# Splitting the first keys two and five, and moving the first FFN chunks behind the fourth slot's value product

## The chip, the cores and the metric

The kernel runs on one core of one Trainium2 chip. TensorE (PE) multiplies matrices and transposes, VectorE (DVE) and ScalarE (ACT) move and transform what it leaves in PSUM, GpSimd (POOL) and SyncE (SP) mostly issue DMAs. The metric is device time of one execution, in microseconds (us), as the median of several runs.

## The reference

```python
q, k, v: (8, 12, 448, 64)          # batch, heads, tokens, head size
scores = q @ k.transpose(0, 1, 3, 2) / sqrt(64) - log(448)
attn   = sigmoid(scores)
x      = (attn @ v).transpose(0, 2, 1, 3).reshape(8 * 448, 768)
out    = (relu(x @ w_gate) * (x @ w_val)) @ w_out      # 768 -> 1536 -> 768
```

Attention has a sigmoid in the place of a softmax, so no row needs a sum before its values are multiplied. The FFN that follows is gated: a gate product, a value product, their elementwise product, and a product down.

## The kernel before, in words

Everything is computed in fp16 with sums in fp32. The order of each engine's instructions is the order of the program text: no scheduler moves anything, and semaphores between the engines follow from the tiles. TensorE's queue therefore runs strictly in the order in which the Python code issues.

A batch has 12 heads, taken in 3 groups of 4. Tokens of a head are cut into 7 chunks of 64. Two heads lie beside each other on the 128 rows, and the transposed queries and keys of a group are held in one tile (`qkT`: 7 chunks of keys, then 7 of queries). Scores are products of 64 x 64 tiles (L238); ScalarE turns them into probabilities `PT` (L186); the value product `pv` (L256) sums over the 7 key chunks, and DVE copies it to `xT` (L183), the FFN's input. Transposes are TensorE matmuls with an identity (L203) into a PSUM bank and a DVE copy to `qkT` (L210).

Batch 0 is treated apart, since nothing else can run beside it at first. Its queries are cut in two halves, of chunks 0 to 3 (256 columns for a head) and 4 to 6 (192). That gives six *slots*, half by group: slots 0 to 2 are groups 0 to 2 with the first half of the queries, slots 3 to 5 the same groups with the second. A slot has four *units* `(i, u)`: units 0 to 2 are two key chunks each, unit 3 is the last one. A unit is scores into one of two score buffers (`pairp`, two PSUM banks each) and one sigmoid over both heads. A buffer must be read by ScalarE before the next but one unit may be written. Four other PSUM banks (`bank`) go round for everything else: transposes, value products, FFN chunks, filler.

What TensorE does between the units is written by hand in the dictionary `after`: what is issued behind unit `(i, u)`. Such work is transposes for later groups, filler matmuls on zeros (`keep_warm(count, columns)`), value products of earlier slots, and FFN chunks. An FFN chunk of the first query half (`gv`, 256 columns) is six matmuls for the gate and six for the value of one of 12 column blocks of 128; DVE takes the maximum with 0 and multiplies. `ffn_mix(1)` issues the next entry of `gv_queue`; the queue's entries for the first half are chunk 0, chunk 1, and one entry of chunks 2 and 3 together (`gv_two`: both gates, then both values).

The first loads are plain fp32 transfers into `ysb` buffers, cast on the chip: keys 0 to 3 of group 0 by SP, queries 0 to 3 and then keys 4 to 6 by ScalarE's queue. All else is loaded and cast by POOL's DMAs in a fixed order: keys and queries of groups 1 and 2, the rest of the queries, the values, then weights (`load_gv`) for chunks 0 and 1, for 2 and 3, batch 1's first group, and so on.

After slot 5 comes batch 1, with scores of all 448 queries at once (the 64x448 matmuls of L238), mixed with the remaining FFN chunks; from there on both versions of the program issue the same.

Of the kernel before, what the change touches and what calls it, by code (L numbers as in the profile page):

```python
# [17 lines left out]
def kernel(  # L18
# [10 lines left out]
    nc = tc.nc  # L29

    B, H, S, D = q.shape
# [3 lines left out]
    P = 128  # L35
    NCH = S // 64
    NDC = DM // P
# [3 lines left out]
    HALVES = ((0, QCUT), (QCUT, NCH))  # L41
# [34 lines left out]
    def bank(name, shape=(P, 512), dtype=FP32):  # L76
        pool, tag = free[0]
        free.rotate(-1)
        return pool.tile(list(shape), dtype, tag=tag, name=name)

    def bank16(name):
        return bank(name, (P, 1024), FP16)
# [35 lines left out]
            )  # L118


    KCUT = 4
    first32 = []
    for src, c0, c1, eng in ((k, 0, KCUT, nc.sync), (q, 0, QCUT, nc.scalar), (k, KCUT, NCH, nc.scalar)):
        ysb = ysbp.tile([P, DM], FP32, tag="ysb", name="ysb")
# [15 lines left out]
    wg = wpool.tile([P, NDC, DF], FP16, name="wg")  # L140
    wv = wpool.tile([P, NDC, DF], FP16, name="wv")
# [26 lines left out]
    xT_tiles = {}  # L168
    hT_tiles = {}

    def keep_warm(count, n=S):
        ps = bank("warm_ps")
        for _ in range(count):
            nc.tensor.matmul(ps[:, 0:n], zeros[:, 0:P], zeros[:, 0:n], start=True, stop=True)
# [14 lines left out]
    def qkT_of(b, g):  # L189
        if (b, g) not in qkT_tiles:  # L190
            qkT_tiles[(b, g)] = qkTp.tile([P, TW, P], FP16, tag="qkT", name="qkT")
        return qkT_tiles[(b, g)]

    def pe_transposes(b, g, ti, c0=0, c1=NCH):
        transposed(b, g, ti, c0, c1)()

    def transposed(b, g, ti, c0, c1):
        t16 = in_tiles[b][ti]
        qkT = qkT_of(b, g)
        trt = bank16("trt")  # L200
        for c in range(c0, c1):
            for h in range(2):
                nc.tensor.transpose(  # L203
                    trt[64 * h : 64 * h + 64, c * P : (c + 1) * P],
                    t16[:, 2 * g + h, c * D : (c + 1) * D],
                    ident[:],
                )

        def copy(a0=c0, a1=c1):
            nc.vector.tensor_copy(  # L210
                qkT[:, ti * NCH + a0 : ti * NCH + a1, :].rearrange("p c x -> p (c x)"),
                trt[:, a0 * P : a1 * P],
            )

        return copy
# [92 lines left out]


    def gv(b, q0, qn, f, act_relu):  # L310
        gv_out(b, q0, qn, f, act_relu, [gv_product(b, q0, qn, f, i) for i in range(2)])

    def gv_two(b, q0, qn, f):
        ps = [[gv_product(b, q0, qn, f + u, i) for u in range(2)] for i in range(2)]
        for u in range(2):
            gv_out(b, q0, qn, f + u, False, (ps[0][u], ps[1][u]))

    def gv_product(b, q0, qn, f, i):
        ps = bank(("g_ps", "v_ps")[i])
        for dc in range(NDC):  # L320
            nc.tensor.matmul(  # L321
                ps[:, 0:qn],
                (wg, wv)[i][:, dc, f * P : (f + 1) * P],
                xT_tiles[b][:, dc, q0 : q0 + qn],
                start=(dc == 0),
                stop=(dc == NDC - 1),
            )
        return ps

    def gv_out(b, q0, qn, f, act_relu, ps):  # L330
        gate_sb = gsbp.tile([P, S], FP32, tag="gsb", name="gate_sb")
        if act_relu:
            nc.scalar.activation(gate_sb[:, 0:qn], ps[0][:, 0:qn], AF.Relu)
        else:
            nc.vector.tensor_scalar(
                out=gate_sb[:, 0:qn], in0=ps[0][:, 0:qn], scalar1=0.0, scalar2=None, op0=AOP.max
            )
        g = b // 2
        if g not in hT_tiles:
            hT_tiles[g] = hTp.tile([P, NFC, 2 * S], FP16, tag="hT", name="hT")  # L340
        o = (b % 2) * S + q0
        nc.vector.tensor_tensor(  # L342
            out=hT_tiles[g][:, f, o : o + qn],
            in0=gate_sb[:, 0:qn],
            in1=ps[1][:, 0:qn],
            op=AOP.mult,
        )
# [316 lines left out]
    gv_queue = deque()  # L664

    def push_gv(b, q0, qn, fs, act_relu=True):
        for f in fs:
            gv_queue.append(lambda f=f: gv(b, q0, qn, f, act_relu))

    def push_first(half, fs, act_relu=True):  # L670
        c0, c1 = HALVES[half]
        push_gv(0, 64 * c0, 64 * (c1 - c0), fs, act_relu)

    def ffn_mix(count, hooks=()):
        hooks = list(hooks)
        for left in range(count, -1, -1):
            while hooks and hooks[0][0] >= left:
                hooks.pop(0)[1]()
            if left:
                gv_queue.popleft()()  # L680


    nc.scalar.activation(gate[:], zeros[:, 0:2], AF.Sigmoid, bias=sig_bias, scale=qk_scale)
    keep_warm(22, 194)
    k16, q16, _ = in_tiles[0]
    nc.vector.tensor_copy(k16[:, 0:2, 0 : KCUT * D], first32[0])
    half = QCUT // 2 * D
    nc.scalar.copy(q16[:, 0:2, 0:half], first32[1][:, :, 0:half])
    nc.vector.tensor_copy(q16[:, 0:2, half : QCUT * D], first32[1][:, :, half:])
    nc.scalar.copy(k16[:, 0:2, KCUT * D : NCH * D], first32[2])  # L690
    transposed(0, 0, 0, 0, 2)()
    other_keys = transposed(0, 0, 0, 2, KCUT)
    transposed(0, 0, 1, 0, 2)()
    transposed(0, 0, 1, 2, QCUT)()
    other_keys()
    keep_warm(2, S // 2)
    slots = [FirstSlot(half * NG + g, g, half) for half in range(2) for g in range(NG)]
    push_first(0, range(0, 2), False)
    gv_queue.append(lambda: gv_two(0, 0, 64 * HALVES[0][1], 2))
    def second_queries():  # L700
        for g in range(1, NG):
            pe_transposes(0, g, 1, QCUT, NCH)

    def first_of_second_group():
        pe_transposes(0, 1, 0, 0, KCUT)
        pe_transposes(0, 1, 1, 0, QCUT)

    def first_of_second_batch():
        pe_transposes(1, 0, 1)
        keys = transposed(1, 0, 0, 0, NCH)  # L710
        keys(0, 3)
        keys(3, NCH)

    def pv_then_queries():
        slots[2].pv()
        second_queries()

    def two_pv():
        slots[3].pv()
        slots[4].pv()  # L720


    after = {
        (0, 0): lambda: pe_transposes(0, 0, 0, KCUT, NCH),
        (0, 1): lambda: keep_warm(4, S // 2),
        (0, 2): first_of_second_group,
        (0, 3): lambda: pe_transposes(0, 1, 0, KCUT, NCH),
        (1, 0): lambda: keep_warm(4, S // 2),
        (1, 1): lambda: pe_transposes(0, 2, 0),
        (1, 2): lambda: pe_transposes(0, 2, 1, 0, QCUT),  # L730
# [2 lines left out]
        (2, 1): lambda: pe_transposes(0, 0, 1, QCUT, NCH),  # L733
        (2, 2): slots[0].pv,
        (2, 3): slots[1].pv,
        (3, 0): pv_then_queries,
        (3, 2): lambda: ffn_mix(1),
        (4, 0): lambda: ffn_mix(1),
        (4, 2): lambda: ffn_mix(1),
        (5, 0): two_pv,  # L740
        (5, 2): first_of_second_batch,
    }
    for i, slot in enumerate(slots):
        for u in range(4):
# [202 lines left out]
```

## Time and profile before

| | us |
|---|---|
| median of 3 runs | 391.79 (391.43 to 391.85) |
| the profiled execution | 392.69 |
| its span, first to last instruction | 390.9 |
| PE busy | 384.7 (98%) |
| DVE busy | 283.4 (73%) |
| ACT busy | 228.4 (58%) |
| first scores of batch 0, of batch 1, from the span's start | 6.31, 29.71 |

Times are in us from the span's start unless a duration is meant. A timeline line gives start, duration of the merged instructions, engine, line of the kernel, operation, output and input tile with shapes, and the count; in brackets the idle time before it and what ended it. PEld is the weight load, which runs ahead of its matmul. Matmuls are pipelined, so that the start of the next line, not the sum of start and duration, says when TensorE went on. A line of DMA issues gives tiles, queue, count, size, and us from issue to landing.

### The profile page before, as it was taken

How to read it: one execution, taken by the hardware profiler on the slowest of the kernel's cores; microseconds unless marked ns; L12 is line 12 of the kernel's file. 1: busy time of each engine (PE TensorE's matmuls, PEld its weight loads, DVE VectorE, ACT ScalarE, POOL GpSimd, SP SyncE). 2: the span in 40 equal slices, each digit the busy share in tenths (PEclk: the TensorE clock that was granted, in tenths of full speed). 3: DMA queues.
4: the chain of work that ended last, by engine and by line, in shares of the span. 5: the costliest groups of instructions: out<-in, count | busy, mean ns of one | idle time of the engine just before them, and what ended most of it. 6: DMA issues, size and time to landing. Idle time of an engine off the chain costs nothing.

```text
span 390.9 us, 8798 instructions
## 1 busy us (share of the span) xinstructions
PE 384.7 (98%) x3504; PEld 218.0 (56%) x3504; DVE 283.4 (73%) x560; ACT 228.4 (58%) x483; POOL 50.1 (13%) x74
## 2 busy tenths in 40 slices
PE   8999999999999999999999999999999999999995
PEld 6678776445455545454555554545455555555663
DVE  3453444358387789999757789999987788999563
ACT  5967786784877755555556774545467354333321
POOL 8643404300320300003000300000000000000000
PEclk9999999999999999999999999999999999999999
DMA  9999997996998992225946696132003220000335
GB/s 174 198 199 204 204 186 120 205 204 111 194 185 166 140 236 37 49 47 58 195 93 115 136 198 108 24 67 41 14 18 74 74 80 2 0 3 0 81 88 155
DMA packets 68985, 43.79 MB, mean 112 GB/s; under 512 B 35664, under 2 KB 65616, under 8 KB 68944
## 3 DMA queue, kind: packets, MB, share of 16 engines
q0 software_dynamic: 30496, 23.24, 39.6%
q1 hardware_dynamic: 37664, 19.24, 24.1%
q10 hardware_dynamic: 784, 0.75, 0.6%
q8 instruction: 27, 0.44, 0.5%
q14 instruction: 14, 0.11, 0.1%
HBM read 47.19 MB, written 11.01 MB: 149 GB/s over the span
## 4 chain that ended last, share of the span: by engine, by line
PE 93%; DMA 4%; DVE 1%; POOL 1%; issue 0%; ACT 0%; POOLq 0%; DVEq 0%; ACTq 0%
PE u L408 33%; PE g L408 16%; PE y L408 10%; PE qk_ps L238 9%; PE pv_ps L256 7%; PE g_ps L321 7%; PE v_ps L321 7%; DMA wv<-in_moe_w_val_dram 3%; DMA k<-in_k_dram 2%; PE ya L369 1%; PE trt L203 1%; PE yb L369 1%; ACT PT L186 0%; DVE ysb L478 0%; POOL wg L148 0%
## 5 line engine op out<-in xcount | busy, mean ns | idle before, releaser
L186 ACT ACTIVATE PT<-qk_ps 128x448 f16<-128x448 f32 (+3 forms) x318 | 151.0, 585 | 75.2 <-PE qk_ps L238 75.0
L408 PEld LDWEIGHTS <-S 128*128 128x128 f16 x558 | 54.6, 98 | 44.7
L620 DVE TENSOR_TENSOR gsb<-g,gsb 128x448 f32<-128x448 f32 x72 | 42.9, 625 | 10.3 <-PE g L408 9.7
L238 PE MATMUL qk_ps<-qkT 64*64 64x448 f16 (+2 forms) x756 | 48.0, 337 | 0.5 <-ACT PT L186 0.3
L342 DVE TENSOR_TENSOR hT<-gate_sb,v_ps 128x256 f16<-128x256 f32 (+2 forms) x36 | 16.4, 465 | 35.5 <-PE v_ps L321 17.9
L408 PEld LDWEIGHTS <-hT 128*128 128x128 f16 x306 | 28.7, 98 | 22.3 <-issue 4.9
L616 ACT COPY gsb<-u 128x448 f32<-128x448 f32 x48 | 25.6, 557 | 24.0 <-PE u L408 22.9
L460 ACT ACTIVATE ysb<-u 128x384 f32<-128x384 f32 x31 | 15.2, 491 | 38.2 <-PE u L408 33.8
L256 PE MATMUL pv_ps<-PT,v 64*64 64x448 f16 (+2 forms) x756 | 37.2, 329 | 0.0
L183 DVE TENSOR_SCALAR xT<-pv_ps 128x448 f16<-128x448 f32 (+2 forms) x53 | 27.8, 567 | 10.9 <-PE pv_ps L256 9.8
L321 PE MATMUL v_ps<-xT,wv 128*128 128x256 f16 (+2 forms) x216 | 33.2, 290 | 0.5 <-DMA wv<-in_moe_w_val_dram 0.5
L321 PE MATMUL g_ps<-xT,wg 128*128 128x256 f16 (+2 forms) x216 | 33.3, 291 | 0.0
L408 PEld LDWEIGHTS <-wg 128*128 128x128 f16 x216 | 20.1, 98 | 21.8 <-issue 4.3
L408 PEld LDWEIGHTS <-wv 128*128 128x128 f16 x216 | 21.1, 98 | 19.7
L238 PEld LDWEIGHTS <-qkT 64*64 64x64 f16 x756 | 18.2, 106 | 21.2 <-issue 14.9
L478 DVE SCALAR_TENSOR_TENSOR ysb<-y,ysb 128x384 f32<-128x384 f32 x29 | 16.1, 556 | 17.9 <-PE y L408 10.4
L256 PEld LDWEIGHTS <-v 64*64 64x64 f16 x756 | 22.3, 107 | 10.6 <-issue 0.8
L408 PE MATMUL u<-T,hT 128*128 128x384 f16 x132 | 25.1, 326 | 0.0
L110 POOL DMA_DIRECT2D k<-in_k_dram x14 | 10.8, 773 | 111.0 <-DVE rel L221 104.2
L321 PEld LDWEIGHTS <-wg 128*128 128x128 f16 x216 | 18.8, 98 | 10.8 <-issue 4.5
L321 PEld LDWEIGHTS <-wv 128*128 128x128 f16 x216 | 20.1, 98 | 8.2 <-DMA wv<-in_moe_w_val_dram 0.8
L408 PE MATMUL u<-xT,wg 128*128 128x448 f16 x108 | 23.5, 354 | 0.0
(78 smaller groups left out, 536.4 us busy)
## 6 DMA issues: line engine op xcount, KB each, us to landing
out_dram<-ysb SPq DMA_DIRECT2D x52, 192.0 KB, 2.9
v<-in_v_dram POOLq DMA_DIRECT2D x8, 336.0 KB, 14.5
v<-in_v_dram POOLq DMA_DIRECT2D x16, 168.0 KB, 14.4
k<-in_k_dram POOLq DMA_DIRECT2D x4, 672.0 KB, 12.0
q<-in_q_dram POOLq DMA_DIRECT2D x4, 672.0 KB, 15.6
k<-in_k_dram POOLq DMA_DIRECT2D x9, 224.0 KB, 11.9
q<-in_q_dram POOLq DMA_DIRECT2D x7, 224.0 KB, 12.2
wo<-in_moe_w_out_dram POOLq DMA_DIRECT2D x1, 1536.0 KB, 12.0
```

The costliest lines, as they stand in the source:

```text
L110: nc.gpsimd.dma_start(t16[:, xs, cs], rows_of(src, b)[:, xs, cs])
L183: nc.vector.tensor_scalar(out=xT, in0=src, scalar1=XSCALE, scalar2=None, op0=AOP.mult)
L186: nc.scalar.activation(PT_ap, ps_ap, AF.Sigmoid, bias=sig_bias, scale=qk_scale)
L238: nc.tensor.matmul(out_of(hh)[o : o + 64, :], qkT[rows, c, cols], qkT[rows, NCH + c0 : NCH + c1, cols], start=True, stop=True, tile_positi ...
L256: nc.tensor.matmul(ps[hh][64 * r : 64 * r + 64, 0:qn], v16[rows, 2 * g + hh, c * D : (c + 1) * D], pieces[c][rows, hh, :], start=(c == 0), ...
L321: nc.tensor.matmul(ps[:, 0:qn], (wg, wv)[i][:, dc, f * P : (f + 1) * P], xT_tiles[b][:, dc, q0 : q0 + qn], start=(dc == 0), stop=(dc == ND ...
L342: nc.vector.tensor_tensor(out=hT_tiles[g][:, f, o : o + qn], in0=gate_sb[:, 0:qn], in1=ps[1][:, 0:qn], op=AOP.mult,)
L408: nc.tensor.matmul(ps[:, 0:n], A[:, k_, :], W[:, k_, :], start=(first and k_ == 0), stop=(k_ == kn - 1), skip_group_check=True,)
L460: nc.scalar.activation(o, ps[:, 0:HM], AF.Copy, scale=OUT_SCALE)
L478: nc.vector.scalar_tensor_tensor(out=o, in0=ps[:, 0:HM], scalar=OUT_SCALE, in1=o, op0=AOP.mult, op1=AOP.add)
L616: by(gs[u][i][:], ps[u][:, 0:S])
L620: nc.vector.tensor_tensor(out=gs[u][i][:], in0=ps[u][:, 0:S], in1=gs[u][i][:], op=AOP.add)
```

## The change

It does four things.

- The first key transfer has 2 chunks (`KCUT = 2`), the second 5. ScalarE casts the second in two steps (chunks 2 and 3, then 4 to 6). Keys 0 and 1 are transposed at the start, keys 2 and 3 behind unit (0, 0), keys 4 to 6 behind unit (0, 1). Before, keys 0 to 3 were transposed at the start in two steps, and 4 to 6 behind (0, 0).
- The fillers of the start are narrower: 22 x 160 columns for 22 x 194, 2 x 112 for 2 x 224, and behind (0, 1) 4 x 112 for 4 x 224.
- From slot 3 on the order behind the units is another. The third slot's value product goes from behind (3, 0) to behind (3, 1), the second queries' transposes from (3, 0) to (3, 2), the fourth slot's value product from (5, 0) to (3, 3), the fifth's from (5, 0) to (4, 3). FFN chunk 0 goes from (3, 2) to (4, 1), chunk 1 from (4, 0) to (4, 3), chunk 2 from (4, 2) to (5, 1), chunk 3 from (4, 2) to (5, 3), behind batch 1's first transposes, which were behind (5, 2).
- Chunks 2 and 3 are issued one after the other, no longer with both gates ahead of both values. `gv_two` goes.

```diff
-    KCUT = 4
+    KCUT = 2
...
-    def gv_two(b, q0, qn, f):
-        ps = [[gv_product(b, q0, qn, f + u, i) for u in range(2)] for i in range(2)]
-        for u in range(2):
-            gv_out(b, q0, qn, f + u, False, (ps[0][u], ps[1][u]))
...
-    keep_warm(22, 194)
+    keep_warm(22, 160)
...
-    nc.scalar.copy(k16[:, 0:2, KCUT * D : NCH * D], first32[2])
-    transposed(0, 0, 0, 0, 2)()
-    other_keys = transposed(0, 0, 0, 2, KCUT)
+    for c0, c1 in ((KCUT, 4), (4, NCH)):
+        nc.scalar.copy(k16[:, 0:2, c0 * D : c1 * D], first32[2][:, :, (c0 - KCUT) * D : (c1 - KCUT) * D])
+    transposed(0, 0, 0, 0, KCUT)()
     transposed(0, 0, 1, 0, 2)()
     transposed(0, 0, 1, 2, QCUT)()
-    other_keys()
-    keep_warm(2, S // 2)
+    keep_warm(2, S // 4)
...
-    push_first(0, range(0, 2), False)
-    gv_queue.append(lambda: gv_two(0, 0, 64 * HALVES[0][1], 2))
+    push_first(0, range(0, 4), False)
...
+    def last_keys():
+        pe_transposes(0, 0, 0, 4, NCH)
+        keep_warm(4, S // 4)
...
     after = {
-        (0, 0): lambda: pe_transposes(0, 0, 0, KCUT, NCH),
-        (0, 1): lambda: keep_warm(4, S // 2),
+        (0, 0): lambda: pe_transposes(0, 0, 0, KCUT, 4),
+        (0, 1): last_keys,
...
-        (3, 0): pv_then_queries,
-        (3, 2): lambda: ffn_mix(1),
-        (4, 0): lambda: ffn_mix(1),
-        (4, 2): lambda: ffn_mix(1),
-        (5, 0): two_pv,
-        (5, 2): first_of_second_batch,
+        (3, 1): slots[2].pv,
+        (3, 2): second_queries,
+        (3, 3): slots[3].pv,
+        (4, 1): lambda: ffn_mix(1),
+        (4, 3): lambda: ffn_then_pv(4),
+        (5, 1): lambda: ffn_mix(1),
+        (5, 3): transposes_then_ffn,
     }
```

`ffn_then_pv(i)` is `ffn_mix(1)` and then `slots[i].pv()`; `transposes_then_ffn` is `first_of_second_batch()` and then `ffn_mix(1)`.

## The prediction

> **What bounds the kernel now.** I read the page first. Its chain of work that ended last is nearly all TensorE:
>
> ```profile
> PE 93%; DMA 4%; DVE 1%; POOL 1%; issue 0%; ACT 0%; POOLq 0%; DVEq 0%; ACTq 0%
> ```
>
> So a microsecond counts if it delays or advances TensorE's queue. The change touches only the first 30 us, up to the first scores of batch 1; behind them both programs issue the same work. I therefore forecast when TensorE reaches those scores (29.71 below). Next I read TensorE's timeline of that stretch:
>
> ```profile
> 6.31 0.59 PE L238 MATMUL qk_ps<-qkT 64*64 64x256 f16 x8
> 6.83 0.36 PE L203 MATMUL trt<-ident,k 128*64 128x128 f16 x6
> 7.12 0.41 PE L238 MATMUL qk_ps<-qkT 64*64 64x256 f16 x8
> ...
> 18.71 0.83 PE L321 MATMUL g_ps<-xT,wg 128*128 128x256 f16 x6
> 20.09 0.83 PE L321 MATMUL v_ps<-xT,wv 128*128 128x256 f16 x6 [0.54 <-DMA wv<-in_moe_w_val_dram]
> ...
> 21.22 0.83 PE L321 MATMUL g_ps<-xT,wg 128*128 128x256 f16 x6
> ...
> 22.63 0.52 PE L238 MATMUL qk_ps<-qkT 64*64 64x192 f16 x16
> ...
> 28.74 1.17 PE L256 MATMUL pv_ps<-PT,v 64*64 64x192 f16 x28
> 29.71 0.76 PE L238 MATMUL qk_ps<-qkT 64*64 64x448 f16 x12
> ```
>
> Two stalls are to be seen. Chunk 0 takes 18.71 to 20.84, 2.13 us, where chunk 1 takes 21.22 to 22.63, 1.41: 0.72 lost to the value weights, which land at 20.04. And the sixth slot's value product has gaps of 0.15 and 0.20 in its weight loads:
>
> ```profile
> 29.25 0.19 PEld L256 LDWEIGHTS <-v 64*64 64x64 f16 x8 [0.15 <-issue]
> 29.63 0.11 PEld L256 LDWEIGHTS <-v 64*64 64x64 f16 x3 [0.20 <-issue]
> ```
>
> It needs the last sigmoids (ScalarE ends them at 29.59), which were issued just before it. Then ScalarE's timeline:
>
> ```profile
> 6.96 10.07 ACT L186 ACTIVATE PT<-qk_ps 128x1024 f16<-128x1024 f32 x12 [1.43 <-PE qk_ps L238]
> 17.22 0.81 ACT L186 ACTIVATE PT<-qk_ps 128x768 f16<-128x768 f32 x1 [0.18 <-PE qk_ps L238]
> ```
>
> In slots 0 to 2 ScalarE sets the pace: twelve sigmoids without a gap, 0.91 us for a full one and 0.63 for the short last, 3.37 a slot. Last, the DMA issues:
>
> ```profile
> ysb<-in_q_dram ACTq DMA_DIRECT2D x1, 256.0 KB, 3.7
> ...
> v<-in_v_dram POOLq DMA_DIRECT2D x2, 168.0 KB, 8.5
> ```
>
> The first queries land at 0.74 + 3.7 = 4.44. The last of batch 0's values are issued at 6.53 and land at about 15.03; the first value product begins at 14.98. It can hardly begin earlier, whatever is gained ahead of it.
>
> **The start.** The first key transfer shrinks from 256 to 128 KB. DMA moves 340 to 385 GB/s from 2.75 to 4.25 us, so 128 KB fewer ahead of the queries are worth about 0.35 us: they land at 4.1 (ends: 4.44 as now, and 3.8). From there: ScalarE's cast 0.47 (4.44 to 4.91), eight query transposes 0.43 (as the keys' now, 4.83 to 5.26), matmul latency 0.31, copy 0.29, steps between engines 0.25: first scores at 5.85 against 6.31, 0.46 earlier (5.55 to 6.2). The filler of 22x160 columns takes 22 x 0.133 = 2.9 us from 1.16 (0.162 each at 194 columns now) and ends at 4.1, just when the small key transposes can start.
>
> **Slot 0.** What is taken off the front is put between the units. The second unit now waits for transposes and the copy of keys 2 to 4, the third for keys 4 to 7; before, only the latter came behind the first unit, with a whole unit between them and their use. From rows: transposes follow a unit by 0.55, the copy follows these by 0.40 (6.83 to 7.23) and takes 0.29 to 0.36, and 0.1 later the scores start. Second unit: 5.85 + 0.55 + 0.40 + 0.29 + 0.1 = 7.2, its sigmoid at 7.75 (now 7.88). Third: 0.40 (a unit at full rate) + 0.40 + 0.36 + 0.1 further, 8.5, sigmoid at 9.0 (now 8.78). ScalarE idles about 0.33 before each. The second group's transposes follow the third unit at 8.9 (now 8.38) and its first scores 1.3 later at 10.2, sigmoid 10.7 (now 10.32). So slot 1 begins 0.4 later though slot 0 began 0.46 earlier. If DVE and TensorE hand over faster than these rows, slot 1 begins 0.1 earlier at best; if the queries do not land earlier, 0.7 later. The middle is taken since each step is priced by a row of its own kind. The fillers (4x112 for 4x224, 2x112 for 2x224) are shorter by 0.2 and 0.1, beside those copies: nothing. ScalarE's split cast (0.40 + 0.51 for 0.51) ends before 6, ahead of the first sigmoid: nothing; SP issues one transfer as before, and POOL's queue is untouched.
>
> **Slots 1 and 2** keep their order, so the first value product moves from 14.87 to about 15.3: +0.45. Were everything early, the values would hold it at 15.0.
>
> **Slot 3.** The third value product moves behind the second unit, which needs the score buffer that ScalarE frees last in slot 2: a wait of about 0.23 that the value product now covers. The query transposes move behind the third unit (their queries land at 16.1, no wait). The fourth slot's value product stands straight behind that slot's last unit. Sigmoids at 17.6, 18.3, 19.0 and 19.7 end at 20.2; without waits it would be through at 20.0, and with the last piece from 20.25 on it leaves at 20.4: +0.40, and all FFN chunks queue behind it. Ends: 0.1 (TensorE late itself) and 0.6.
>
> **Chunks.** Chunk 0 starts at 20.85, its value weights at 21.5, 1.5 after landing: -0.72. Chunks 2 and 3 (weights down by 24.08) come after that and need no pairing. Four single chunks instead of two singles and a pair put one more return to scores in, 4 x 1.41 against 2 x 1.41 + 2.72: +0.1. Chunk 3 stands before the sixth slot's value product and covers its sigmoids: -0.36. Batch 1's queries land at 26.32 and are transposed at about 26.9: no wait, 0.5 of cover; without that cover the stall would come back here.
>
> **Sum:** -0.72 - 0.36 + 0.45 + 0.23 + 0.40 + 0.1 = +0.1, nil within its steps. Cross-check forward: 20.4 + 0.45 + 1.41 + 0.38 + 1.41 + 0.58 + 0.46 + 1.41 + 0.38 + 0.91 (transposes) + 1.41 + 0.58 = 29.8 against 29.71. Against the profiled execution (span 390.9, itself 392.69) that is 392.7; its time is 0.9 above the median of 391.79, so the forecast for the median is 391.8. Slot 1's ends (-0.5, +0.3) and the stall's (-0.3, +0.2), not all at once, give its own range: 391.3 to 392.3. 0.2%, about what a measurement of this kernel can tell from no change, is 0.78 us.
>
> **Rivals.** *TensorE stays at half rate* (slower). Matmuls run slowly up to about 6.65: eight scores take 0.59 at 6.31 and 0.41 at 7.12, a transpose lasts 314 ns before and 219 after, 5.5 us after the first filler. The filler now ends 0.6 earlier, and waits for the query cast and the copies open holes between 4.1 and 6.6. If the rise needs a denser stretch than that, slot 0 runs at half rate: two units cost 0.18 more each, 26 transposes 0.026 more each (0.054 against 0.028), 1.0 together, some 0.1 of it beside ScalarE: +0.9, 392.7. For it: nothing but filler fills that stretch. Against: the holes are about 0.6 of 2.5 us. It decides once the rise comes later than about 9 us. The Trainium skill (TensorE: Matmul & The Clock Gate, Part 1) has the full clock come only after a busy window of some 3.4 us, in free-running windows; its Part 4 says that transposes do not count as busy. By that rule the window before 6.65 would fail more easily and the next chance be near 10.1, an estimate by that page; that the row switched at 6.65 in spite of transposes speaks for some tolerance.
>
> *The early start carries through* (faster): the values land earlier too, or the key copies hide, so that the 0.46 reaches the value products: -0.72 - 0.36 + 0.40 - 0.46 + 0.1 = -1.0, 390.8. For it: both stalls are real, and their removal needs only that slot 3 stays on time. Against: values at 15.03 move with the bytes in front of them, which are the same.
>
> *The queries set the start* (the change does not do what it says): they land at 4.44 as now, first scores 6.2, and slot 0's two waits remain: +0.3 on the forecast, 392.1.
>
> **Chances.** Forecast 0.43, half rate 0.28, early start 0.19, queries 0.10. Faster: the early start and a trace of the forecast's lower end, 0.20. Slower: half rate and the worst of the queries' case with the long stall, 0.32. The rest, 0.48, is within 0.2%. The range takes in all prices, with 0.3 beyond the half-rate sum for a later rise: 390.8 to 393.0.
>
> **What the profile after would show.** Right: first scores near 5.85; idle ScalarE before the second and third sigmoid; the second group's first sigmoid near 10.7; no wait on the value weights; a gap in the fourth slot's value product; batch 1's scores near 29.8. Wrong: ScalarE without gaps in slot 0 and the first value product before 14.9; slow transposes after 7 us; batch 1's scores more than 0.8 away from 29.71; or a difference made behind 30 us, which I exclude.

## The result, and the profile after

| | us |
|---|---|
| before, median of 6 runs | 391.73 (391.43 to 391.85) |
| after, median of 6 runs | 394.83 (393.08 to 396.00) |
| ratio | 1.0077 (95% interval 1.0052 to 1.0102) |
| after, the profiled execution | 394.32, span 392.6 |

The change makes the kernel 0.8% slower, 3.1 us, and the runs spread over 3 us where those of before lie within 0.5. In the profiled execution batch 1's scores begin at 31.43 where the first trace of before has 29.71. Behind them nothing differs: profiled time less the start of those scores is 363.0 in before (392.69 - 29.71), 362.9 in after (394.32 - 31.43), and 362.9 to 363.0 in eleven of the twelve experiments (363.2 in the other, after with 22 instructions fewer). So all of it lies in the first 31 us, as the prediction had it.

The page's chain of after is TensorE's as before, with ScalarE's sigmoids now in it:

```profile
PE 94%; ACT 2%; DVE 1%; DMA 1%; issue 1%; DVEq 0%; ACTq 0%
```

TensorE's timeline of after, the start and slots 3 to 5 (lines left out are marked ...):

```profile
5.88 0.41 PE L238 MATMUL qk_ps<-qkT 64*64 64x256 f16 x8 [0.27 <-DVE qkT L210]
...
6.92 0.41 PE L238 MATMUL qk_ps<-qkT 64*64 64x256 f16 x8 [0.39 <-DVE qkT L210]
...
8.14 0.64 PE L238 MATMUL qk_ps<-qkT 64*64 64x256 f16 x8
...
15.77 0.96 PE L256 MATMUL pv_ps<-PT,v 64*64 64x256 f16 x28
...
16.64 0.96 PE L256 MATMUL pv_ps<-PT,v 64*64 64x256 f16 x28
...
19.66 1.15 PE L256 MATMUL pv_ps<-PT,v 64*64 64x192 f16 x28
20.62 0.36 PE L238 MATMUL qk_ps<-qkT 64*64 64x192 f16 x7
22.15 0.41 PE L238 MATMUL qk_ps<-qkT 64*64 64x192 f16 x9 [1.18 <-issue]
22.49 0.83 PE L315 MATMUL g_ps<-xT,wg 128*128 128x256 f16 x6
23.16 0.82 PE L315 MATMUL v_ps<-xT,wv 128*128 128x256 f16 x6
...
30.83 0.77 PE L256 MATMUL pv_ps<-PT,v 64*64 64x192 f16 x28
31.43 0.74 PE L238 MATMUL qk_ps<-qkT 64*64 64x448 f16 x12
```

The wait on the value weights is gone (23.16 follows 22.49 at full pace), and so are the gaps in the sixth slot's value product (0.60 us from 30.83 to 31.43). Two things are new. Inside unit (4, 0), after 7 of its 8 matmuls, TensorE stands 1.18 us and the profile names no releaser ("issue"): units (4, 0) and (4, 1) take 20.62 to 22.49, 1.87 us, where two such units take 0.45 before (18.26 to 18.71):

```profile
18.26 0.52 PE L238 MATMUL qk_ps<-qkT 64*64 64x192 f16 x16
18.71 0.83 PE L321 MATMUL g_ps<-xT,wg 128*128 128x256 f16 x6
```

And the third unit's scores take 0.64 where the first two took 0.41: the rate falls back. At full rate eight scores of 256 columns take 0.41, at half rate 0.64. The windows of after show the fall in the granted clock (PEclk, the third number from the end):

```profile
core 0: us, PE busy (x) PEld busy (x) DVE busy (x) ACT busy (x) POOL busy (x), PEclk, DMA share, GB/s
7.00:7.50 0.50, 0.50 (x14) 0.26 (x14) 0.00 (x0) 0.48 (x2) 0.50 (x2) 0.91 1.25 197
7.50:8.00 0.50, 0.50 (x10) 0.32 (x4) 0.27 (x1) 0.50 (x1) 0.50 (x2) 0.50 1.41 192
...
10.50:11.00 0.50, 0.50 (x11) 0.20 (x9) 0.36 (x1) 0.29 (x1) 0.50 (x1) 0.68 1.26 203
11.00:11.50 0.50, 0.50 (x12) 0.32 (x8) 0.00 (x0) 0.38 (x1) 0.34 (x2) 1.00 1.25 197
```

A mean of 0.91 over a window of 0.5 us, with 0.5 behind the fall, means that the fall came 0.09 us before the window's end, at 7.41; 0.68, that the rise came at 10.82. ScalarE's timeline shows the price, idle time ahead of the third, fourth and fifth sigmoid, where before had none:

```profile
8.84 1.02 ACT L186 ACTIVATE PT<-qk_ps 128x1024 f16<-128x1024 f32 x1 [0.44 <-PE qk_ps L238]
10.19 0.60 ACT L186 ACTIVATE PT<-qk_ps 128x512 f16<-128x512 f32 x1 [0.33 <-PE qk_ps L238]
11.12 9.37 ACT L186 ACTIVATE PT<-qk_ps 128x1024 f16<-128x1024 f32 x12 [0.33 <-PE qk_ps L238]
```

The DMA issues of after: in this execution the first queries land at 0.74 + 3.8, no earlier than in the first trace of before.

```profile
ysb<-in_q_dram ACTq DMA_DIRECT2D x1, 256.0 KB, 3.8
...
ysb<-in_k_dram SPq DMA_DIRECT2D x1, 128.0 KB, 3.4
```

### The profile page after: what moved, and what is told of

Read it like the earlier page. It is cut to its first block, busy times and chain, and to the rows that moved or that the text cites. A ratio compares the mean times of both kernels' runs of the same rounds, so it can differ in the third digit from the quotient of the medians.

```text
span 392.6 us, 8798 instructions
## 1 busy us (share of the span) xinstructions
PE 384.8 (98%) x3504; PEld 217.7 (55%) x3504; DVE 283.4 (72%) x560; ACT 228.8 (58%) x484; POOL 50.0 (13%) x74
## 4 chain that ended last, share of the span: by engine, by line
PE 94%; ACT 2%; DVE 1%; DMA 1%; issue 1%; DVEq 0%; ACTq 0%
PE u L399 33%; PE g L399 16%; PE y L399 10%; PE qk_ps L238 9%; PE pv_ps L256 8%; PE g_ps L315 8%; PE v_ps L315 7%; ACT PT L186 2%; PE trt L203 1%; PE ya L360 1%; DMA ysb<-in_q_dram 1%; PE yb L360 1%; DVE ysb L469 0%; DVE qkT L210 0%; DVE S L390 0%
## 5 line engine op out<-in xcount | busy, mean ns | idle before, releaser
L399 PEld LDWEIGHTS <-wv 128*128 128x128 f16 x216 | 21.1, 98 | 19.8
L238 PEld LDWEIGHTS <-qkT 64*64 64x64 f16 x756 | 18.3, 106 | 22.8 <-issue 16.4
L469 DVE SCALAR_TENSOR_TENSOR ysb<-y,ysb 128x384 f32<-128x384 f32 x29 | 16.1, 556 | 17.9 <-PE y L399 10.4
L315 PEld LDWEIGHTS <-wg 128*128 128x128 f16 x216 | 18.7, 98 | 10.8 <-issue 4.5
```

The lines of the kernel that those rows point to most:

```text
L238: nc.tensor.matmul(out_of(hh)[o : o + 64, :], qkT[rows, c, cols], qkT[rows, NCH + c0 : NCH + c1, cols], start=True, stop=True, tile_positi ...
L315: nc.tensor.matmul(ps[-1][:, 0:qn], wt[:, dc, f * P : (f + 1) * P], xT_tiles[b][:, dc, q0 : q0 + qn], start=(dc == 0), stop=(dc == NDC - 1),)
L399: nc.tensor.matmul(ps[:, 0:n], A[:, k_, :], W[:, k_, :], start=(first and k_ == 0), stop=(k_ == kn - 1), skip_group_check=True,)
L469: nc.vector.scalar_tensor_tensor(out=o, in0=ps[:, 0:HM], scalar=OUT_SCALE, in1=o, op0=AOP.mult, op1=AOP.add)
```

## The experiments

Theory A: TensorE takes its instructions in blocks that come by DMA, and the new order runs through one faster than the next arrives. The trace has a queue for such blocks, "q8 instruction". The page of after counts 27 packets and 0.44 MB on it, for 7008 weight loads and matmuls, that is about 260 a packet; one packet falls into the window from 19.7 to 19.8:

```profile
q8 instruction: 27, 0.44, 0.5%
...
q8 instruction: 1, 0.02, 60.9%
```

Theory B: the new start leaves TensorE too idle, and it is at half rate in slot 0. All times are medians beside before on the same chip (391.74 to 391.83).

### The order alone, the start alone

The first kernel has after's order on before's start. The second has after's start on before's order:

```diff
-    KCUT = 4
-    keep_warm(22, 194)
+    KCUT = 2
+    keep_warm(22, 160)
...            (casts, transposes and the two other fillers as in after; slots 3 to 5 as in before)
```

> The start of before (keys 4 + 3, wide fillers) with the order of after from slot 3 on. Theory A (TensorE reaches the end of a block of its instructions before the next block is there; the order of after runs through those instructions faster): a gap of about 1.2 us in the first scores of slot 4, before the last matmul of unit (4, 0), as in after; time about 392.9, some 1.2 over before. Theory B (the cost is in the start: TensorE falls back to half rate in slot 0): no gap there, the order costs nothing, 391.5 to 391.9. In both the first sigmoid of the second group stays near 10.3.

> The start of after (keys 2 + 5, narrow fillers, keys transposed between the units) with the order of before from slot 3 on. Theory A: no gap of 1 us before the batch-1 scores; only what slot 0 loses, 0.4 to 0.8, less what the wait for the value weights takes up: 391.7 to 392.5. Theory B: half of the rise or more, 393 to 395, with matmuls at half rate between 7 and 11 us and times that spread over a microsecond or more.

Measured: the order alone 393.18 (392.86 to 393.23; 1.0032, 1.0020 to 1.0044). Its gap is where after has it:

```profile
19.70 0.36 PE L238 MATMUL qk_ps<-qkT 64*64 64x192 f16 x7
21.00 0.43 PE L238 MATMUL qk_ps<-qkT 64*64 64x192 f16 x9 [0.94 <-issue]
```

The start alone: 393.30, but in two groups, six runs from 391.51 to 392.70 and six from 393.90 to 394.78 (1.0034, 1.0015 to 1.0053), with no gap in slot 4. Its trace, a run of 394.34, shows scores at 0.64 up to 12.53 and at 0.41 from 13.80. Both theories hold, each for its half of the change: the order costs every run 1.1 to 1.5, the start costs some runs 2 to 3 and others nothing that can be told.

### After with 22 instructions fewer, and after again

```diff
-    keep_warm(22, 160)
+    keep_warm(11, 320)
```

> After with the first filler as 11 matmuls of 320 columns in the place of 22 of 160: the same array time, 22 fewer instructions ahead (a weight load and a matmul for each of 11). Theory A: the gap stays with the instruction count and so moves 22 instructions down the work, from the last matmul of unit (4, 0) past unit (4, 1) (16) to the fourth matmul of FFN chunk 0's gate product, give or take one, and is as long or up to 0.4 shorter (that stretch has four slow matmuls more before the block's end). Rival (a wait of that unit for its score buffer or for ScalarE): the gap stays in unit (4, 0). Time within 1 of after.

> After unchanged, for a second trace, since its runs spread from 393.08 to 396.00. Theory A: the gap stands before the same matmul, with another length (0.5 to 4). Theory B: the gap is as before, and the half-rate stretch is longer or elsewhere. Time 393 to 396.

The gap moved, to before the third gate matmul of chunk 0:

```profile
22.47 0.39 PE L315 MATMUL g_ps<-xT,wg 128*128 128x256 f16 x2
23.68 0.60 PE L315 MATMUL g_ps<-xT,wg 128*128 128x256 f16 x4 [0.81 <-issue]
```

Counting TensorE's weight loads and matmuls from the first filler, that is the 704th; in after the 8th matmul of unit (4, 0) is the 704th as well. The gap belongs to the count, not to the unit. After again (393.08; six runs from 392.93 to 393.12, two at 395.33 and 395.96) has it at the same matmul, 1.05 long, in the profiled run of 395.96, which also stayed at half rate far longer:

```profile
8.97 0.64 PE L238 MATMUL qk_ps<-qkT 64*64 64x256 f16 x8
...
12.79 0.64 PE L238 MATMUL qk_ps<-qkT 64*64 64x256 f16 x8
...
14.17 0.41 PE L238 MATMUL qk_ps<-qkT 64*64 64x256 f16 x8
...
17.46 0.96 PE L256 MATMUL pv_ps<-PT,v 64*64 64x256 f16 x28
```

The first value product begins at 17.46, against 15.77 in the first trace of after. So after's runs fall into groups as well: 393.0 to 393.1, 394.1 to 394.3 (the first trace, where the rate falls back once) and 395 to 396 (this trace, where it rises only near 14). No run of the lowest group was profiled; that its rate rises in time is inferred from the order alone, which has the same time at full rate. After with fewer instructions: 393.62 (three runs at 393.0 to 393.1, three at 394.1 to 395.6; the profiled one, at 395.55, at half rate up to about 13.7). The filler's time there is the same and its count is half, and the groups stay: they do not come from the count.

### The fillers

The fifth kernel is after with the three fillers of before, the sixth is before with the three of after:

```diff
 # e5, on after                        # e6, on before
-    keep_warm(22, 160)                -    keep_warm(22, 194)
+    keep_warm(22, 194)                +    keep_warm(22, 160)
...
```

> After with the fillers of before (22 x 194, 2 x 224, 4 x 224) and its own key split. Theory B1 (the narrower fillers leave TensorE too idle for the rise to full rate): full rate by 7 us in every run, runs within 0.5 of each other near 393.1, the gap of about 1.1 in slot 4 stays. Theory B2 (the waits for keys between the units alone do it): half rate until 10 us or later in part of the runs, which spread over 2 us as those of after (393 to 396).

> Before with the fillers of after (22 x 160, 2 x 112, 4 x 112) and nothing else. Theory B1: part of the runs stay at half rate past 7 us: a spread of 1 us or more, 391.5 to 394.5. Theory B2: as before, 391.4 to 392.3, all runs together.

Wide fillers bring after to 393.34 with all runs from 393.03 to 393.57: the spread of 3 us is gone, and the gap in slot 4 stays (1.09). That is theory B1. But narrow fillers alone cost before nothing that was measured: 391.86 (391.43 to 392.89; 1.0003, 0.9993 to 1.0013), though in its trace the scores still take 0.64 at 8.37 and are down to 0.41 by 10.51. The trace does what B1 expected of it, the times do not: those of before beside it spread as wide (391.36 to 392.75). To lose 2 us and more takes the narrow fillers and the waits for keys between the units together; what either does alone to the rate stays partly open.

> Before with the key split of after (2 + 5 chunks, transposes between the units), but the fillers of before. Theory: the split by itself costs or gains next to nothing once TensorE comes to full rate in time: 391.5 to 392.1, runs within 1.4 of each other as those of before. Rival (the waits for the keys between the units cost by themselves): 392.2 or more.

The eleventh kernel is the second with the wide fillers: 391.98 (391.71 to 392.55; 1.0005, 0.9996 to 1.0014). The key split by itself is worth nothing that these runs can tell (-0.2 to +0.55 us).

### Filler in the gap, and before again

On the first kernel:

```diff
-        (3, 3): slots[3].pv,
+        (3, 3): pv_then_filler,        # slots[3].pv(), then keep_warm(5): five of 448 columns
```

> The first experiment's kernel (the start of before, the order of after) with five filler matmuls of 448 columns, 0.93 us of TensorE's time, behind the fourth slot's value product, just ahead of the gap. Theory A (the next block of instructions comes at its own time, some 5 us after the one ahead was begun): the filler fills the gap, which shrinks from 0.94 to 0.0 to 0.2, and the time stays at 393.0 to 393.4. Rival (a fixed cost at that place, whatever runs ahead): the gap stays near 0.9 and the time rises by 0.9 to about 394.1.

> Before unchanged, for a second trace, since its first profiled execution (392.69) is above all its timed ones. Theory A: TensorE begins the block of instructions that holds slot 4 near 16 us and reaches the block after it only near 22.5, with the wait for the value weights between, so that no gap of its own is seen. Theory B: full rate by about 7 us. Time 391.4 to 392.7.

The filler cost nothing: 393.17 (392.84 to 393.35) against 393.18, and what is left of the gap is 0.20, in the weight loads, between the 2nd and the 3rd matmul of unit (4, 0); the 3rd is the 704th instruction here. Units (4, 0) and (4, 1) take 0.76 (20.54 to 21.30), 0.3 more than without a wait:

```profile
20.54 0.11 PEld L238 LDWEIGHTS <-qkT 64*64 64x64 f16 x2 [0.37 <-issue]
20.85 0.30 PEld L238 LDWEIGHTS <-qkT 64*64 64x64 f16 x14 [0.20 <-issue]
```

So the next instruction comes at a time of its own. Six traces give that time, and before again stands beside them. The 448th instruction (256 ahead of the 704th, taken as the block's beginning) stands near the beginning of the second value product; its time is estimated by counting along that line (in after the 4th of the 28 matmuls from 16.64 on), to about 0.1 us. The packet's time is the beginning of the 0.1 us window in which it starts:

| | 448th | packet | 704th goes on | after the 448th |
|---|---|---|---|---|
| order alone | 15.84 | 18.5 | 21.00 | 5.2 |
| after | 16.75 | 19.7 | 22.15 | 5.4 |
| after, wide fillers | 15.81 | 18.6 | 21.12 | 5.3 |
| after again | 18.44 | 21.1 | 23.71 | 5.3 |
| 22 fewer | 18.46 | 21.3 | 23.68 | 5.2 |
| filler in the gap | 15.51 | 18.3 | 20.85 | 5.3 |
| before again | 15.34 | 17.9 | reached at about 21.5 | 6.2, no gap |

Before gets there later than the block does, because two FFN chunks stand on the way. The other traces with chunk 0 in its old place get there later too, 5.7 to 6.6 us after the 448th, and none has the gap (the first trace of before, the start alone, the narrow fillers, and the tenth to twelfth kernel). That the unnamed wait is for instructions is inferred from this: it keeps to the count, to 5.2 to 5.4 us, and to the packet 2.4 to 2.6 ahead. Why the packet comes when it does was not varied: from 15 to 24 us the DMA engines were busy throughout in every trace, at 198 to 199 GB/s. The Trainium skill (Runtime: NRT & Kernel Launch, section Instruction fetch mechanics) says that TensorE's instructions are refilled in blocks of 256 while the one ahead runs, and that the cost of a boundary is mostly hidden. The traces agree on the block (0.44 MB in 27 packets, about 260 weight loads and matmuls a packet) and not on the hiding: 0.8 to 1.2 us stand open here.

Before again ran in 391.38, and its scores of batch 1 begin at 28.44, 1.3 earlier than in the first trace. Its rate was full from the first transposes on, and the value weights came earlier, so that chunk 0 lost little:

```profile
17.96 0.83 PE L321 MATMUL g_ps<-xT,wg 128*128 128x256 f16 x6
18.81 0.83 PE L321 MATMUL v_ps<-xT,wv 128*128 128x256 f16 x6
19.57 0.44 PE L238 MATMUL qk_ps<-qkT 64*64 64x192 f16 x12
```

17.96 to 19.57 is 1.61, 0.20 above the 1.41 of a chunk without waits. The trace from which the prediction was made was a slow one in both respects.

### Chunk 0 ahead of the fourth slot's value product

On the first kernel:

```diff
-        (3, 3): slots[3].pv,
-        (4, 1): lambda: ffn_mix(1),
+        (3, 3): lambda: ffn_then_pv(3),
```

> The first experiment's kernel (the start of before, the order of after) with FFN chunk 0 ahead of the fourth slot's value product in the place of behind unit (4, 1). Theory A: the chunk's 12 slow matmuls stand inside the block that was run through too fast, so the block's end (24 instructions earlier in the work, in the last matmuls of that value product) is reached 1.4 later; the gap falls from 0.94 to 0.3 or less and the value product's wait for its sigmoids goes: 391.7 to 392.3. Rival (the later place of the value products, not the instructions, costs the time): 393.0 to 393.4 as before.

It came out at 393.35 (393.32 to 393.67), as the rival had it. The unnamed gap did what theory A said: it falls from 0.94 to 0.30, in the weight loads, and again stands at the 704th instruction, now in the 24th matmul of that value product:

```profile
20.46 0.47 PEld L256 LDWEIGHTS <-v 64*64 64x64 f16 x23 [0.21 <-issue]
21.23 0.13 PEld L256 LDWEIGHTS <-v 64*64 64x64 f16 x5 [0.30 <-issue]
```

The 448th stands at about 16.05 here and the packet at 18.7, so the 704th goes on 5.2 after the one and 2.5 after the other, as in the table. But slot 4 is now four units in a row with nothing between them, and ScalarE, which had stood idle during chunk 0, holds them up:

```profile
22.72 0.36 PE L238 MATMUL qk_ps<-qkT 64*64 64x192 f16 x8 [0.80 <-ACT PT L186]
23.42 0.28 PE L238 MATMUL qk_ps<-qkT 64*64 64x192 f16 x4 [0.34 <-ACT PT L186]
```

One wait was exchanged for another. The edit took away cover as well as adding it, so its time doesn't separate the theories; the place of the gap speaks for A.

### Two pairs of chunks

Before with both pairs of chunks issued gates first, and the value products and transposes between them:

```diff
-    push_first(0, range(0, 2), False)
-    gv_queue.append(lambda: gv_two(0, 0, 64 * HALVES[0][1], 2))
+    for f in (0, 2):
+        gv_queue.append(lambda f=f: gv_two(0, 0, 64 * HALVES[0][1], f))
...
+        (4, 0): slots[3].pv,
         (4, 2): lambda: ffn_mix(1),
+        (5, 0): slots[4].pv,
+        (5, 3): first_of_second_batch,
```

> Before with chunks 0 and 1 as a pair behind (3, 2), both gates ahead of both values, and chunks 2 and 3 as a pair behind (4, 2); the fourth slot's value product behind (4, 0), the fifth's behind (5, 0), batch 1's first transposes behind (5, 3). If the wait for the value weights and the sixth slot's wait for its sigmoids are what before still loses (0.2 to 0.7 and 0.36), 391.0 to 391.6. If the instruction blocks come too late for this order, a gap of 0.3 to 1 near 22 us and 391.7 to 392.5.

> The tenth and the eleventh experiment's edits together: if their effects add, the tenth's time plus the eleventh's difference from before, within 0.3.

Both are slower than before: 392.71 (1.0023, 1.0013 to 1.0032) and 393.03 (1.0030, 1.0020 to 1.0041), so the eleventh kernel's edit adds 0.3 where it added 0.15 to before, within what was expected. The tenth lies above both of its expectations. TensorE no longer waits for the weights, the sixth slot's value product has no gap, and none is seen at the 704th instruction, but TensorE now waits 0.9 us in three places (0.26, 0.26 and 0.35) for ScalarE to free a score buffer. No experiment beat before.

## Why the prediction was wrong

It forecast no change, 391.8 within 390.8 to 393.0; it is 394.83. Of the 3.1 us about 1.4 is the order, most of it (1.2) a wait for instructions that the prediction does not have, and the rest is half rate, a rival that it priced too low. How many runs the second one takes is chance as far as these runs tell: five of the first six, two of the eight of after again, whose median is 393.08 and so still beyond the range.

**The step that is missing** is in the part on slot 3: "the fourth slot's value product stands straight behind that slot's last unit" was priced for its sigmoids, and whether TensorE's instructions are there in time for so many short ones in a row was not priced at all. A value product of 64 x 64 tiles goes through 56 instructions in 0.77 us, 14 ns each; an FFN chunk through 24 in 1.41, 59 ns each. After moves the chunks out of the stretch from the 448th to the 704th instruction and runs it in 4.2 us (16.75 to 20.98); before needs 6.2, and the block comes after 5.2 to 5.4. The cost is 1.2 (order alone, 19.70 to 21.37 for two units less 0.45) to 1.4 (after). It was hidden in the trace of before by work, and nothing in that trace named it; the instruction queue's packets were there to be read.

**The step that was mis-sized** is the first: "0.72 lost to the value weights". That was the first trace's loss; the second has 0.20, and the eleventh kernel, with the same order, has none (18.58 to 19.99, 1.41). The value weights land between 18.4 and 19.2 in twelve of the fourteen traces; 20.04 is one of the two late ones. A single execution's DMA landings were taken for the kernel's, and partly counted twice: the 0.9 taken off for the median already held some of that loss. "It can hardly begin earlier", said of the first value product, rests on the same landings: in before again it begins at 14.36, with the last values down by 14.01.

**The other terms of the order held.** Order alone against before again, from the first value product to batch 1's scores: 30.31 - 14.87 = 15.44 against 28.44 - 14.36 = 14.08, 1.36 more. The prediction's terms with measured sizes: fourth slot's sigmoids +0.35 (forecast 0.40; 18.75 to 19.70, against 0.60), the score buffer with small rests about +0.25 (0.23), one return more +0.1, sixth slot's sigmoids -0.37 (0.36), weights -0.20 (0.72), and the block +1.22: 1.35.

**The start.** "They land at 4.1" was too early: in the first trace of after the queries landed at 4.5, as before. But over all traces the smaller key transfer does bring them forward. They land at 4.24 to 4.53, 4.38 in the mean, in the seven traces with two key chunks first, and at 4.48 to 4.71, 4.62 in the mean, in the seven with four: 0.24 earlier, where 0.35 was forecast. First scores come at 5.77 to 6.05, 5.89 in the mean, against 5.88 to 6.34, 6.20 in the mean: 0.31 earlier, forecast 0.46. So the step was right in direction and about two thirds in size, and the rival *the queries set the start* was right for one trace only. That after's 5.88 lies so near the 5.85 forecast is in part luck: its rate was full by then, and before again, with the large transfer, has 5.88 too. ScalarE's idle time was forecast before the second and the third sigmoid; it came before the third, fourth and fifth (0.44, 0.33, 0.33). For the +0.45 that stood in the sum for the split, the eleventh kernel, with wide fillers, shows +0.15, and its interval of -0.2 to +0.55 leaves the size open.

**Half rate** was the rival with 0.28, and it happens: by their times in six of twelve runs of the start alone, two of eight of after again, and five of the first six of after, in one of which the trace shows it as a fall from 7.41 to 10.82. Its price was too low, 0.9 for a rise near 10; the rise came as late as 13.5 to 14 and the cost was 2 to 3 us, because the point "later than about 9 us" was followed no further than one more stretch. The first rise, by the first entry of the clock record kept with each trace, comes at 3.9 to 7.2 in the nine traces with wide fillers, and at 4.0, 9.8, 13.5, 13.7 and 14.0 in the five with narrow or fewer ones. The runs of after without it, at 393.0 to 393.1, are 1.3 above before, about the block's price. The Trainium skill (TensorE: Matmul & The Clock Gate, Part 1) has the rate decided over free-running windows of about 3.4 us; the fall at 7.41 and the rise at 10.82 are 3.41 apart, which agrees. A phase that is free would explain why equal runs differ; no run here sets it. Whether transposes count, as its Part 4 denies, no run here separates.

## What to carry to other kernels

When an order is changed, count instructions as well as microseconds: a stretch of small-tile matmuls ran through them four times as fast as the large ones here (14 against 59 ns), and with the DMA engines busy throughout the next 256 took over 5 us to come, so keep slow instructions among the fast ones. Size the filler ahead of the first real work by the run in which the rate rises last, not by when the data arrive; here runs that spread in groups 1 to 3 us apart were the sign that it was too thin. And take a second trace of before ahead of booking a DMA wait as a gain.

## What the runs showed of the hardware that was not expected

- TensorE stood 0.8 to 1.2 us at its 704th weight load or matmul, with no releaser in the profile, in the five traces in which it got there 4.2 to 4.4 us after the 448th, and went on 5.2 to 5.4 us after it; five filler matmuls (0.93 us) in that place were free.
- The same program ran its first scores at full rate or, in other executions, at half rate up to about 14 us, 2 to 3 us apart in time; the rate also fell back in one trace, for 3.41 us, after a start with holes.
- The granted clock in the windows says 1.00 through 5 to 13 us of after again, where transposes take 314 ns and scores 0.64 for eight: the first half-rate stretch shows only in the durations, a later fall in that column too.
- In one order the removal of a wait led straight to ScalarE: with two score buffers, units in a row come no faster than a sigmoid each 0.70 us.
